# Turning the memory at a step's end in two parts, with the sum copied by ScalarE

## The chip, the cores and the metric

The kernel runs on one core of a Trainium2 chip. The metric is the device time of one execution in microseconds (us). The executions shown beside each other are of the same program on the same inputs; the figure is their median. One more execution was recorded by the hardware profiler, and all durations below come from that one.

The engines are TensorE (PE, with its weight loads listed apart as PEld), VectorE (DVE), ScalarE (ACT), GpSimd (POOL) and SyncE (SP). In this kernel SP only issues transfers of weights.

## The reference, cut to what matters

Two branches read the same x and are mixed by a gate. Branch A is attention in a sliding window of 256. Branch B runs over 64 segments of 32 tokens; each segment sees 8 memory rows that the segment before it has made, so the 64 steps follow one another.

```python
# S = 2048, Dm = 640, H = 32 heads, Dh = 192, M = 8 memory rows, seg_len = 32
mem = mem0
for s in range(n_seg):                                   # 64 steps
    xs = x[:, s * seg_len:(s + 1) * seg_len, :]
    h = concatenate([mem, xs], axis=1)                   # 40 rows x 640
    q, k, v = h @ Wq, h @ Wk, h @ Wv                     # 640 -> 32 heads x 192
    p = softmax(where(mask, q @ k.T * Dh ** -0.5, -1e9))
    o = (p @ v) @ Wo                                     # 40 rows x 640
    mem = o[:, :M, :]                                    # the next step's memory
    outs.append(o[:, M:, :])
return g * a + (1 - g) * concatenate(outs, axis=1)       # a: branch A, g: gate
```

## The kernel before, in words

Branch A comes first, and then the parts of branch B that need no memory. From about 434 us on the 64 steps run, the function branch_B.

All operations of all steps are first recorded by `sc.op(engine, duration, latency, function, reads, writes, ...)` in a planner, the class Sched. The order on PE is written out by hand: the string STEP names the work of one step, and it ends with "oa3 ob3 m", after which the next step's "k0 q0 k1 ..." begins. The order on SP is the order of recording. On DVE, ACT and POOL the planner chooses among ready operations by rank, with the duration and latency that were written beside each operation. The program is then emitted in that order. Each engine works through its own instructions in order.

The heads are worked in 4 groups of 8. For a group g the step has projections q, k and v (line 773), their turns tq and tk (line 797), scores s, the turn p of the probabilities, values pv, and the projection back, in two halves oa and ob (line 968). A projection is 5 pieces of the contraction, kt = 0 to 4, each with 4 small matmuls. Its stationary operand is `hT`, the step's input turned: 128 partitions x 5 pieces x 32 columns. Of a piece's 32 columns 0 to 7 are the memory rows and the others are tokens that a POOL transfer brings in (line 703). The last 8 tokens of a segment don't depend on the memory; their projections were made for all steps ahead.

[...]21 pieces a step, of 384 KB (q, k, v) or 320 KB (o), are streamed on SP's queue into a ring of 5 buffers, `b_w`. A transfer into a buffer is issued when PE has read the piece that lay there. The pieces read first in a step are one of k0, one of q0, one of k1 and one of q1.

The end of a step is a short serial path:

1. The projection back has summed into one PSUM bank, `ps_o`, 128 partitions x 320 in fp32: partitions 0 to 63 hold the columns 0 to 319 of o, partitions 64 to 127 the columns 320 to 639. The rows 0 to 7 of each half are the new memory.
2. DVE copies the sum into a bf16 tile, `osum` (line 977; the tile comes from the pool OT).
3. PE turns the memory rows by 10 small matmuls with an identity, 5 pieces x 2 halves, into a PSUM tile `mem_ps` (line 989, the operation "m" of STEP).
4. DVE copies `mem_ps` into columns 0 to 7 of all 5 pieces of the next step's `hT` (line 994).
5. PE begins k0 of the next step.

Beside this path POOL stores osum (line 999) and fetches branch A's rows `ga` (line 1000); DVE mixes both later (line 1004, placed by the planner after a copy of the next step), and POOL stores the result (line 1008). PSUM tiles of the pool "tr" have two buffers that the turns and `mem_ps` use in rotation.

Of the kernel before, what the change touches and what calls it, by code (L numbers as in the profile page):

```python
# [8 lines left out]
FP32 = mybir.dt.float32  # L9
BF = mybir.dt.bfloat16  # L10
ALU = mybir.AluOpType
ACT = mybir.ActivationFunctionType
# [3 lines left out]
MEM = 8  # L16
# [377 lines left out]
P = 128  # L394
KT = 5
D = 640
# [273 lines left out]
def branch_B(ctx, tc, xin, mem0, weights, ring, c, omg_sb, ga_dram, b_dram, outf, hold, held, rest):  # L670
    nc = tc.nc
    nseg = xin.shape[0]
    scale = float(192) ** -0.5
    still, ident, mask, mk_m, mk_x, mk_z = c.still, c.ident, c.mask, c.mk_m, c.mk_x, c.mk_z
    kept = KEPT

    sb = {
        "w": (RING, [P, PIECE]), "tok": (3, [P, 384]), "vtok": (1, [P, 384]), "K02": (1, [P, 4, 2, L]),
        "PTm": (1, [P, 2, 4, L]), "Pm": (1, [P, 4, SEG]), "xg": (2, [P, 2, 12, MEM]), "xv": (1, [P, 384]), "hT": (2, [P, KT, SEG]),
# [6 lines left out]
    sc = Sched({"rest": len(held)} | {t: n for t, (n, _) in sb.items()} | {t: n for t, (n, _) in kept.items()} | ps)  # L686

    def tile_of(b, shape=None, dtype=BF, name=None):
        t = b["tag"]
        if b["tile"] is None:  # L690
            if t in kept:
                b["tile"] = still[t][b["n"] % kept[t][0]]
            elif t in sb:
                b["tile"] = pools[t].tile(sb[t][1], BF, name=f"b_{t}", tag=t)
            else:
                b["tile"] = pools[t].tile(shape, dtype, name=name or f"p_{t}", tag=t)
        return b["tile"]

    def load_x(s):
        hb = sc.buf("hT")  # L700

        def f():
            nc.gpsimd.dma_start(tile_of(hb)[:].rearrange("p k t -> p (k t)"), xin[s, :, 0:KT * SEG])
        return hb, sc.op("POOL", 540, 5000, f, writes=[hb])
# [16 lines left out]
    def pieces(kind, g, ms=range(5)):  # L721

        out = {}
        for m in ms:
            u = (kind, g, m)
            if u in weights.streamed:
                b = out[m] = sc.buf("w")
                sc.op("SP", 0.753 * weights.width(kind), 3000, lambda b=b, u=u: weights.load(u, tile_of(b)[:, 0:weights.width(u[0])], nc.sync), writes=[b])
        return out

    def w_of(kind, g, m, bufs):
        return bufs[m]["tile"] if m in bufs else weights.tiles[kind, g, m]
# [15 lines left out]
    hts = {0: load_x(0)}  # L748
# [3 lines left out]
    def f_m0():  # L752
        t = tile_of(tp, [P, KT, MEM], BF, "tp0")
        for kt in range(KT):
# [4 lines left out]
          writes=[hts[0][0]], after=[hts[0][1]])  # L759
    made, tails = {}, {}  # L760

    def chunk(kind, s, g):
        if s == 0 and kind == "v":
            load_slow(g)
        hT = hts[s][0]
        b = sc.buf("mm")
        wb = pieces(kind, g)

        def f(kt):
            t = tile_of(b, [P, 512], FP32, f"ps_{kind}")  # L770
            w = w_of(kind, g, kt, wb)
            for j in range(4):
                nc.tensor.matmul(t[32 * j:32 * j + 32, 0:384], lhsT=tile_of(hT)[:, kt, :], rhs=w[:, j * 384:(j + 1) * 384],  # L773
                                 start=(kt == 0), stop=(kt == KT - 1), tile_position=(0, 32 * j))
        for kt in range(KT):
            sc.op("PE", 160, 330, lambda kt=kt: f(kt), reads=[hT] + [wb[m] for m in wb if m == kt], writes=[b], name=(kind, s, g, kt), mode=32)
        tok = sc.buf("vtok" if kind == "v" else "tok")

        def ev():
            src, dst = b["tile"][:, 0:384], tile_of(tok)[:]  # L780
            if kind == "v":
                src = src.rearrange("p (a e b) -> p a b e", a=2, b=3)
                dst = dst.rearrange("p (a b e) -> p a b e", a=2, b=3)
            nc.scalar.copy(dst, src)  # L784
        sc.op("ACT", 480, 50, ev, reads=[b], writes=[tok])
        made[kind, s, g] = tok
# [165 lines left out]
    def oproj(kind, s, g):  # L952

        ms = PARTS[kind]
        OT = made["O", s, g]
        if g == 0 and kind == "oa":
            obufs[s] = sc.buf("o")
        o_b = obufs[s]
        wb = pieces("o", g, ms)

        def f(m):
            t = tile_of(o_b, [P, 512], FP32, "ps_o")
            for n in range(2):
                i, b = divmod(2 * m + n, 3)
                c = (4 * b + i) * L
                for h in range(2):
                    w = w_of("o", g, m, wb)[:, n * D + h * (D // 2):n * D + (h + 1) * (D // 2)]
                    nc.tensor.matmul(t[64 * h:64 * h + 64, 0:D // 2], lhsT=OT["tile"][:, c:c + 64], rhs=w,  # L968
                                     start=(g == 0 and m == 0 and n == 0), stop=(g == 3 and m == 5 and n == 1),
                                     tile_position=(0, 64 * h), skip_group_check=True)  # L970
        for m in ms:
            sc.op("PE", 273, 200, lambda m=m: f(m), reads=[OT] + [wb[n] for n in wb if n == m] + [slow[u] for u in slow if s == 0 and u == ("o", g, m)],
                  writes=[o_b], name=("o", s, g, m), mode=64)
        if g < 3 or kind == "oa":
            return
        osum = sc.buf("OT")
        sc.op("DVE", 492, 55, lambda: nc.vector.tensor_copy(tile_of(osum)[:, 0:D // 2], o_b["tile"][:, 0:D // 2]), reads=[o_b], writes=[osum])  # L977
        made["osum", s] = osum

    def finish(s):  # L980

        osum = made.pop(("osum", s))
        b = sc.buf("tr")

        def f():
            t = tile_of(b, [P, KT, MEM], FP32, "mem_ps")
            for kt in range(KT):
                for h in range(2):
                    nc.tensor.matmul(t[64 * h:64 * h + 64, kt, :], lhsT=osum["tile"][:, kt:D // 2:KT], rhs=ident[:, 64 * h:64 * h + MEM],
                                     start=(kt == 0), stop=True, tile_position=(0, 64 * h), skip_group_check=True)  # L990
        sc.op("PE", 360, 222, f, reads=[osum], writes=[b], name=("m", s), mode=64)
        if s + 1 < nseg:
            hT, xl = hts[s + 1]
            sc.op("DVE", 200, 55, lambda: nc.vector.tensor_copy(tile_of(hT)[:, :, 0:MEM], b["tile"][:]), reads=[b], writes=[hT], after=[xl])
        ga, rows = sc.buf("ga"), slice(s * SEG, (s + 1) * SEG)
        half = lambda t, h: t[rows, h * (D // 2):(h + 1) * (D // 2)]
        mine = lambda t, h: t[64 * h + MEM:64 * h + L, 0:D // 2]
        for h in range(2):
            sc.op("POOL", 500, 3000, lambda h=h: nc.gpsimd.dma_start(half(b_dram, h), mine(osum["tile"], h)), reads=[osum])
            sc.op("POOL", 500, 5000, lambda h=h: nc.gpsimd.dma_start(mine(tile_of(ga), h), half(ga_dram, h)), writes=[ga])  # L1000

        def mix(after):
            def f_r():
                nc.vector.scalar_tensor_tensor(out=ga["tile"][:], in0=osum["tile"][:, 0:D // 2], scalar=omg_sb[:, s:s + 1], in1=ga["tile"][:],  # L1004
                                               op0=ALU.mult, op1=ALU.add)
            sc.op("DVE", 552, 60, f_r, reads=[osum], writes=[ga], after=[after])
            for h in range(2):
                sc.op("POOL", 500, 3000, lambda h=h: nc.gpsimd.dma_start(half(outf, h), mine(tile_of(ga), h)), reads=[ga])  # L1008
        made["mix"] = mix
        if s + 1 == nseg:  # L1010
            mix(None)
# [3 lines left out]
    for n in names:  # L1015
        kind, s = n[:2]
# [6 lines left out]
        elif kind in "qkv":  # L1023
            chunk(kind, s, n[2])
        elif kind in PARTS:
            oproj(kind, s, n[2])
        else:
            make[kind](s, n[2])
    with tc.manual_schedule():
        parts = []  # L1030
        for n in names:
            if n[0] in PARTS:
                parts += [("o",) + n[1:] + (m,) for m in PARTS[n[0]]]
            elif n[0] in KINDS:
                parts += [n + (m,) for m in range(KT)]
            else:
                parts.append(n)
        return sc.run([("m0", 0)] + parts)


PARTS = {"oa": range(3), "ob": range(3, 6)}
RING = 5
EARLY = 24
LAST = 11
# [9 lines left out]
def kernel(  # L1054
# [40 lines left out]
    units = [lambda u=u: weights.load_resident(pre, u, nc.sync) for u in early]  # L1095
    ring = wctx.enter_context(tc.tile_pool(name="b_w", bufs=RING))
    first = {}
# [78 lines left out]
    with ExitStack() as bctx:  # L1176
        rest = bctx.enter_context(tc.tile_pool(name="b_rest", bufs=1))
        branch_B(bctx, tc, xin, mem0, weights, ring, step_c, omg_sb, ga_dram, b_dram, outf, holds[0], last[HOLD:], rest)
# [41 lines left out]
```

## Time and profile before

| what | value |
|---|---|
| median of 5 executions | 2074.73 us |
| lowest and highest of them | 2064.33 and 2082.09 us |
| the profiled execution's own time | 2074.79 us |
| its span, first to last instruction | 2073.1 us |
| granted TensorE clock, mean over the span | 0.993 |
| busy share of the span: PE, DVE, ACT, POOL | 92%, 51%, 44%, 35% |
| bytes moved by the transfer engines | 593.83 MB, mean 286 GB/s |
| copy of the sum, DVE, line 977 | 64 times 492 ns |
| small products of the turn, PE, line 989 | 640 times, 217 ns each at the median, overlapping |
| copy into the next input, DVE, line 994 | 63 times 200 ns |

The span is nearly all of the profiled execution's time: 1.7 us lie around it. The profiled execution lies at the median of the others, so a difference worked out against the one may be read against the other.

How to read it: busy shares are means over the whole span, which holds branch A too. In the 64 steps PE and the transfer engines are both busy most of the time, and neither share says alone which one the end waits for. A matmul's own duration is longer than its share of the engine, since several are in flight at once.

### The profile page before, as it was taken

Reading aid. Unit: us, or ns where it says so; the run is one execution under the profiler, and the core shown is the slowest. Engines: PE = TensorE matmul, PEld = TensorE weight load, DVE = VectorE, ACT = ScalarE, POOL = GpSimd, SP = SyncE. Lnnn points to the kernel's source line nnn. Section 1 sums busy time; section 2 is a strip of 40 time slices with the busy share of each in tenths; the row PEclk is TensorE's granted clock in tenths of the full one; section 3 lists DMA queues with packets and bytes.
Section 4 is the critical chain, followed back from the end, with each engine's and each line's share of the span. In section 5 each row is a group of like instructions: output and inputs, shape, how many; then the busy total and the mean of one; then the engine's idle time right before and its main releaser. Section 6 shows DMA issues by size and latency. Waiting matters only on the chain.

```text
span 2073.1 us, 92142 instructions
## 1 busy us (share of the span) xinstructions
PE 1915.6 (92%) x39670; PEld 1410.8 (68%) x39670; DVE 1049.5 (51%) x3338; ACT 919.7 (44%) x1885; POOL 719.1 (35%) x2008
## 2 busy tenths in 40 slices
PE   7999999989999999999899999999999999989997
PEld 6878878756666666666666666666666666666665
DVE  4888853334444444445444444444444444444444
ACT  3788832234444444444444444444444444444443
POOL 4121121233334333333333333333333333333333
PEclk8999999999999999999999999999999999999999
DMA  4232149789999999999999999999999999999997
GB/s 137 78 89 69 45 109 349 205 285 327 333 323 333 328 322 320 329 326 333 320 332 331 321 331 326 327 332 334 331 314 337 327 318 337 333 323 318 332 330 263
DMA packets 251153, 593.83 MB, mean 286 GB/s; under 512 B 39528, under 2 KB 59120, under 8 KB 250736
## 3 DMA queue, kind: packets, MB, share of 16 engines
q1 hardware_dynamic: 219248, 540.07, 75.0%
q0 software_dynamic: 31488, 47.78, 8.7%
q8 instruction: 313, 5.13, 1.0%
q14 instruction: 104, 0.85, 0.1%
HBM read 558.33 MB, written 29.37 MB: 283 GB/s over the span
## 4 chain that ended last, share of the span: by engine, by line
PE 60%; DMA 25%; issue 7%; DVE 5%; ACT 3%; SPq 0%; POOL 0%; POOLq 0%; DVEq 0%; ACTq 0%
DMA b_w<-in_B_Wo_dram 10%; PE ps_q L773 10%; DMA b_w<-in_B_Wv_dram 10%; PE ps_k L773 10%; PE ps_o L968 8%; PE ps_v L773 6%; PE t_psum L584 4%; DMA b_w<-in_B_Wk_dram 4%; PE qk_ps L138 3%; PE t_psv L602 3%; PE tr_q L797 2%; PE S_ps L853 2%; PE tr_k L797 2%; PE s_ps L236 2%; PE ps_pv L935 2%
## 5 line engine op out<-in xcount | busy, mean ns | idle before, releaser
L773 PEld LDWEIGHTS <-b_hT 128*32 128x32 bf16 x15360 | 372.6, 96 | 273.6 <-issue 59.4
L968 PEld LDWEIGHTS <-b_OT 128*64 128x64 bf16 x6144 | 370.8, 110 | 57.7 <-issue 35.2
L784 ACT CAST b_tok<-ps_k 128x384 bf16<-128x384 f32 x256 | 122.4, 478 | 347.5 <-PE ps_k L773 338.8
L773 PE MATMUL ps_q<-w_q,b_hT 128*32 128x384 bf16 x4096 | 257.9, 329 | 2.1 <-issue 2.1
L773 PE MATMUL ps_k<-w_k,b_hT 128*32 128x384 bf16 x4096 | 245.6, 328 | 0.0
L968 PE MATMUL ps_o<-hold,b_OT 128*64 128x320 bf16 x2560 | 236.3, 300 | 0.0
L919 DVE TENSOR_TENSOR b_PTm<-PT_ps,marks 128x320 bf16<-128x320 f32 x256 | 125.9, 492 | 203.9 <-PE PT_ps L907 203.9
L968 PE MATMUL ps_o<-b_w,b_OT 128*64 128x320 bf16 x1792 | 206.4, 300 | 23.7 <-DMA b_w<-in_B_Wo_dram 22.0
L824 DVE TENSOR_TENSOR b_Kz<-tr_k,marks 128x256 bf16<-128x256 bf16 x256 | 108.1, 422 | 236.8 <-PE tr_k L797 230.7
L773 PE MATMUL ps_v<-w_v,b_hT 128*32 128x384 bf16 x3584 | 212.6, 327 | 0.0
L239 ACT ACTIVATE pt<-s_ps 128x1024 bf16<-128x1024 f32 x180 | 183.4, 1025 | 57.3 <-PE s_ps L236 54.3
L946 ACT CAST b_OT<-ps_pv 128x480 bf16<-128x480 f32 x256 | 142.9, 558 | 139.5 <-PE ps_pv L942 139.5
L784 ACT CAST b_vtok<-ps_v 128x384 bf16<-128x384 f32 x256 | 122.5, 478 | 158.8 <-PE ps_v L773 158.0
L718 POOL DMA_DIRECT2D b_xg<-xin x256 | 141.9, 554 | 83.5 <-POOL b_QT L810 51.4
L968 PE MATMUL ps_o<-w_o,b_OT 128*64 128x320 bf16 x1792 | 170.1, 300 | 0.0
L829 POOL COPY b_K<-b_xg 128x64 bf16<-128x64 bf16 x256 | 60.6, 237 | 306.9 <-PE S_ps L853 306.9
L806 ACT COPY b_QT<-tr_q 128x384 bf16<-128x384 bf16 x256 | 123.4, 482 | 87.8 <-PE tr_q L797 87.6
L784 ACT CAST b_tok<-ps_q 128x384 bf16<-128x384 f32 x256 | 122.9, 480 | 87.5 <-PE ps_q L773 87.2
L773 PE MATMUL ps_v<-b_w,b_hT 128*32 128x384 bf16 x1536 | 131.1, 331 | 30.8 <-DMA b_w<-in_B_Wv_dram 29.9
L1008 POOL DMA_DIRECT2D out_dram<-b_ga x128 | 63.5, 497 | 261.5 <-DVE b_ga L1004 251.7
L977 DVE CAST b_OT<-ps_o 128x320 bf16<-128x320 f32 x64 | 31.5, 492 | 212.3 <-issue 205.9
L797 PEld LDWEIGHTS <-b_tok 128*64 128x64 bf16 x3072 | 108.6, 111 | 41.4 <-issue 23.2
(141 smaller groups left out, 3712.0 us busy)
## 6 DMA issues: line engine op xcount, KB each, us to landing
b_w<-in_B_Wv_dram SPq DMA_DIRECT2D x384, 384.0 KB, 4.8
b_w<-in_B_Wo_dram SPq DMA_DIRECT2D x448, 320.0 KB, 4.8
b_w<-in_B_Wk_dram SPq DMA_DIRECT2D x256, 384.0 KB, 5.0
b_w<-in_B_Wq_dram SPq DMA_DIRECT2D x256, 384.0 KB, 5.1
xin<-hold POOLq DMA_DIRECT2D x8, 1536.0 KB, 11.9
b_xg<-xin POOLq DMA_DIRECT2D x256, 48.0 KB, 4.5
w_q<-in_B_Wq_dram SPq DMA_DIRECT2D x16, 384.0 KB, 3.8
w_k<-in_B_Wk_dram SPq DMA_DIRECT2D x16, 384.0 KB, 3.6
```

What stands on the lines that cost most here:

```text
L239: nc.scalar.activation(out=pt, in_=sp[:], func=ACT.Exp, scale=scale)
L584: self.nc.tensor.matmul(pt[:, bb, :], lhsT=w[kt][:, c:c + P], rhs=self.xTb[:, kt, t0:t0 + hs * MEM], start=(kt == 0), stop=(kt == KT - 1))
L718: sc.op("POOL", 540, 5000, lambda: nc.gpsimd.dma_start(tile_of(b)[:].rearrange("p i b t -> p (i b t)"), xin[s, :, c:c + 192]), writes=[b])
L773: nc.tensor.matmul(t[32 * j:32 * j + 32, 0:384], lhsT=tile_of(hT)[:, kt, :], rhs=w[:, j * 384:(j + 1) * 384], start=(kt == 0), stop=(kt == ...
L784: nc.scalar.copy(dst, src)
L797: nc.tensor.transpose(t[64 * a:64 * a + 64, k, :], tok["tile"][:, c:c + 64], ident[:], tile_position=(0, 64 * a))
L806: nc.scalar.copy(dst, tq["tile"][:].rearrange("p b (j t) -> p b j t", t=SEG))
L824: nc.vector.tensor_tensor(out=tile_of(Kz)[:, :, :, 0:SEG], in0=src, in1=mk_z.unsqueeze(1).unsqueeze(3).to_broadcast([P, 4, 2, SEG]), op=AL ...
L919: nc.vector.tensor_tensor(out=tile_of(PTm)[:], in0=src.to_broadcast([P, 2, 4, L]), in1=mk_m.unsqueeze(1).unsqueeze(3).to_broadcast([P, 2, ...
L946: sc.op("ACT", 560, 50, lambda: nc.scalar.copy(tile_of(OT)[:, 0:12 * L], o["tile"][:, 0:12 * L]), reads=[o], writes=[OT])
L968: nc.tensor.matmul(t[64 * h:64 * h + 64, 0:D // 2], lhsT=OT["tile"][:, c:c + 64], rhs=w, start=(g == 0 and m == 0 and n == 0), stop=(g == ...
L1008: sc.op("POOL", 500, 3000, lambda h=h: nc.gpsimd.dma_start(half(outf, h), mine(tile_of(ga), h)), reads=[ga])
```

## The change

The ten small products become two groups: the pieces 0 and 1 (4 products) and the pieces 2 to 4 (6 products), each into a PSUM tile of its own. Each group has its own DVE copy into its pieces of hT. The copy of the sum goes from DVE to ACT. The order on PE stays: both groups stand where the one group stood, between ob3 and the next k0.

```diff
         osum = sc.buf("OT")
-        sc.op("DVE", 492, 55, lambda: nc.vector.tensor_copy(tile_of(osum)[:, 0:D // 2], o_b["tile"][:, 0:D // 2]), reads=[o_b], writes=[osum])
+        sc.op("ACT", 430, 50, lambda: nc.scalar.copy(tile_of(osum)[:, 0:D // 2], o_b["tile"][:, 0:D // 2]), reads=[o_b], writes=[osum])
         made["osum", s] = osum
...
-        b = sc.buf("tr")
-
-        def f():
-            t = tile_of(b, [P, KT, MEM], FP32, "mem_ps")
-            for kt in range(KT):
-                for h in range(2):
-                    nc.tensor.matmul(t[64 * h:64 * h + 64, kt, :], lhsT=osum["tile"][:, kt:D // 2:KT], rhs=ident[:, 64 * h:64 * h + MEM],
-                                     start=(kt == 0), stop=True, tile_position=(0, 64 * h), skip_group_check=True)
-        sc.op("PE", 360, 222, f, reads=[osum], writes=[b], name=("m", s), mode=64)
-        if s + 1 < nseg:
-            hT, xl = hts[s + 1]
-            sc.op("DVE", 200, 55, lambda: nc.vector.tensor_copy(tile_of(hT)[:, :, 0:MEM], b["tile"][:]), reads=[b], writes=[hT], after=[xl])
+
+        def turn(i, kts):
+            b = sc.buf("tr")
+
+            def f():
+                t = tile_of(b, [P, KT, MEM], FP32, "mem_ps")
+                for kt in kts:
+                    for h in range(2):
+                        nc.tensor.matmul(t[64 * h:64 * h + 64, kt, :], lhsT=osum["tile"][:, kt:D // 2:KT], rhs=ident[:, 64 * h:64 * h + MEM],
+                                         start=(kt == kts[0]), stop=True, tile_position=(0, 64 * h), skip_group_check=True)
+            sc.op("PE", 72 * len(kts), 222, f, reads=[osum], writes=[b], name=("m", s, i), mode=64)
+            if s + 1 < nseg:
+                hT, xl = hts[s + 1]
+                c = slice(kts[0], kts[-1] + 1)
+                sc.op("DVE", 150, 55, lambda: nc.vector.tensor_copy(tile_of(hT)[:, c, 0:MEM], b["tile"][:, c]), reads=[b], writes=[hT], after=[xl])
+        for i, kts in enumerate(TURNS):
+            turn(i, kts)
...
+            elif n[0] == "m":
+                parts += [n + (i,) for i in range(len(TURNS))]
...
+TURNS = (range(2), range(2, KT))
```

## The prediction

> **What bounds the kernel now.** I read the windows of the steps first, for the balance of PE and transfers; then the timeline of one step's end; then the waits; then the chain of waits. In the windows view, columns are length, busy time by engine, granted clock, transfer share and GB/s.
>
> ```profile
> core 0: us, PE busy (x) PEld busy (x) DVE busy (x) ACT busy (x) POOL busy (x), PEclk, DMA share, GB/s
> 1736.37:1760.38 24.01, 23.07 (x526) 16.64 (x526) 12.17 (x43) 10.57 (x24) 9.63 (x29) 1.00 0.98 343
> ...
> 1530.09:1557.98 27.89, 25.06 (x526) 17.68 (x526) 12.17 (x43) 10.61 (x24) 9.63 (x29) 0.94 0.92 304
> ...
> 465.00:2065.00 1600.00, 1478.08 (x33109) 1059.92 (x33100) 766.53 (x2708) 666.51 (x1512) 601.83 (x1752) 1.00 0.96 327
> ```
>
> The first row is the shortest step, 24.01 us; the second the longest, at a lower clock. Over all of them PE is busy 1478 of 1600 us (92%) and the transfers hold 0.96. Both are near their ends. Every step has the same end, here one of them:
>
> ```profile
> 1022.73 0.44 PE L968 MATMUL ps_o<-b_w,b_OT 128*64 128x320 bf16 x4
> 1023.27 0.49 DVE L977 CAST b_OT<-ps_o 128x320 bf16<-128x320 f32 x1 [2.90 <-issue]
> 1023.81 0.46 PEld L989 LDWEIGHTS <-b_OT 128*64 128x64 bf16 x10 [0.97 <-DVE b_OT L977]
> 1023.81 0.54 PE L989 MATMUL mem_ps<-ident,b_OT 128*64 128x8 bf16 x10 [0.64 <-DVE b_OT L977]
> 1024.05 1.00 POOL L999 DMA_DIRECT2D b_dram<-b_OT  x2 [2.51 <-DVE b_OT L977]
> 1024.40 0.20 DVE L994 CAST b_hT<-mem_ps 128x40 bf16<-128x40 f32 x1 [0.64 <-PE mem_ps L989]
> ...
> 1024.65 0.35 PE L773 MATMUL ps_k<-b_w,b_hT 128*32 128x384 bf16 x4 [0.30 <-DVE b_hT L994]
> ```
>
> From the end of the last back projection (1022.73 + 0.44 = 1023.17) to the next k0 (1024.65) PE does nothing but ten small products: 1.48 us, 63 times, 93 us in all. The steps' waits say what else PE waits for:
>
> ```profile
> PE mem_ps L989 <- DVE b_OT L977: 40.8, 63, 1.0
> PE ps_v L773 <- DMA b_w<-in_B_Wv_dram: 26.7, 50, 1.7
> PE ps_o L968 <- DMA b_w<-in_B_Wo_dram: 21.5, 46, 1.5
> PE ps_k L773 <- DVE b_hT L994: 16.1, 54, 0.3
> PE ps_k L773 <- DMA b_w<-in_B_Wk_dram: 10.8, 13, 1.4
> ```
>
> Beside the step's end PE waits 26.7 + 21.5 + 10.8 = 59 us for weights, nearly 1 us a step. The shortest step has no such wait. So which one sets the end? The chain of waits through the steps passes the small products ("PE mem_ps L989") at 49 of the 63 ends. At the other 14 it goes past them through a weight transfer, mostly of Wk, issued before the step's end and landing behind it:
>
> ```profile
> 1249.03 7.34 DMA b_w<-in_B_Wk_dram
> 1256.37 0.04 issue
> 1256.41 0.51 PE ps_k L773 x8
> ```
>
> **The copy of the sum, from DVE to ACT.** DVE takes 492 ns for 320 columns. ACT's rows for fp32 from PSUM into bf16 are 478 ns for 384 columns (line 784) and 558 ns for 480 (line 946): 80 / 96 = 0.833 ns a column, so 478 - 64 x 0.833 = 425 ns for 320. The gain is 67 ns. From below ACT's 128x256 copy bounds it, 379 ns (line 568), from above the 478. The Trainium skill (VectorE: DVE Perf Modes, section on the TRN2 errata) gives for PSUM to SBUF 120 cycles + columns at 0.96 GHz on VectorE and 172 + columns at 1.2 GHz on ScalarE: 458 and 410 ns, a gain of 48. By the page this part is worth 63 x 48 = 3.0 us, by the rows 63 x 67 = 4.2; I take the rows. ACT is free: its last work before is line 946 at 1020.74 for 0.56, its next is line 784 at 1025.70. Behind the waiting copy on ACT stands only that evacuation of k0, which needs the copy anyway. ACT starts behind PE as soon as DVE does (0.04 us after ps_pv in the same step), and PE started 0.05 us behind ACT's line 946. POOL's stores of line 999 now wait for ACT and come 67 ns sooner; their order and SP's are unmoved.
>
> **The turn in two groups.** Ten products span 0.54 us, one 217 ns: (540 - 217) / 9 = 36 ns apart. Four of them end after 3 x 36 + 217 = 325 ns, 215 sooner than ten. The copy of 40 columns takes 200 ns, that of the sum 492 for 320: 292 / 280 = 1.04 ns a column and 158 fixed. 16 columns take 175 ns, 24 take 183. The first copy then ends 215 + 25 = 240 ns sooner. Counted from the first product (1023.81 in the example): first copy 0.38 to 0.55, k0 at 0.60 instead of 0.84. The second group is queued between, on PE, but is done at 0.54; the second copy starts behind the first at 0.59, ends at 0.77 and frees PE at 0.82. k0's pieces 0 and 1 need no more than the first copy; a piece takes 0.17 to 0.18 us, so piece 2 is due at 0.60 + 0.35 = 0.95. The second copy is covered by 0.13 us; without that cover it would cost what it is late, piece by piece. It is the thing that is late next. What the trace doesn't show is a wait in mid-group before piece 2 that is already met: at best 0, at worst the restart after a real wait, which I read from the chain: 20 products of k0 take 1.00 us behind the copy, of other groups 0.81, so 0.19. I take 0, since the loads run ahead of the products. The extra DVE copy (63 x 183 ns = 11.5 us busy) lies where DVE waits for tr_k for 3.01 us; it holds up nothing. The products and the pool "tr" get one more buffer use a step; the PSUM tile that the second group needs was last read at the turn of p3, over 3 us earlier.
>
> **The sum.** 67 + 240 = 307 ns an end, 63 x 0.307 = 19.3 us if every end counted. At the 14 ends that the chain passes by, nothing comes of it: 49 x 0.307 = 15.0 us. A step that starts sooner also finds its first four streamed pieces (k0, q0, k1, q1, within 3.3 us) landed later by comparison. Of them 13 products of k waited already. I let five more ends go that way, a choice, roughly one in ten of the 49: 44 x 0.307 = 13.5 us. 2074.8 - 13.5 = 2061.3; I say **2061 us**.
>
> The rule against it: the Trainium skill (Perfetto Trace Analysis, Identifying the Most-Contended Engine) would have one optimize the engine of the highest occupancy first. By that the transfers at 0.96 set the step and this change, which moves no byte less, gives 0: 2074.8. The rows say more. A mean step ((2040.2 - 463.8) / 62 = 25.43 us, from the first and the last copy of line 994) leaves 4% of transfer time idle, 1.0 us; the shortest leaves 2%, 0.5 us. 0.5 us can be taken up, more than 0.31. And the longest step has one of the lowest shares (0.92), which a pure limit of the transfers wouldn't give. So I take most of the sum, not all.
>
> **The rivals.** *Transfers hide it.* The saving turns into waits for weights, in the head of the step or at the v and o pieces, where most waits already are. For it: 0.96, and a wait in most steps. Against it: 49 of 63 ends on the chain. It gives 0 to 6 us: about 2071. *The halves aren't separate*: k0 waits for both copies after all, since hT is one tile. Then k0 starts at 0.82 instead of 0.84, 87 ns an end, 49 x 0.087 = 4 us: 2070.5. In the built program piece 2's load carries a wait of its own, so this is unlikely. *Broken heads*, the slower side: each of the first four streamed pieces that PE now overtakes costs a stall with its 0.19 us of restart. One stall takes back part, 0.307 / 0.19 = 1.6 new stalls a step take all; three would make 0.57 - 0.31 = 0.26 us a step, 63 x 0.26 = 16 us slower, 2091. For it: k products waited 13 times. Against it: q products waited once, and the shortest steps have none. *All of it counts*: 19.3 us, 2055.5.
>
> **How the numbers follow.** A change under 0.5% (10.4 us, so from 2064.4 to 2085.2) is about what a measurement here can't tell from none. Chances: the forecast 0.50 (2056 to 2067, six sevenths of it below 2064.4), all of it 0.10, hidden 0.20, not separate 0.05, broken heads 0.15. Faster 0.43 + 0.10 = 0.53; same 0.07 + 0.20 + 0.05 + 0.04 = 0.36; slower 0.11, since a mild form of broken heads stays within the bound. The range 2048 to 2080 leaves out most of broken heads and little else.
>
> **What would show it.** Line 977 on ACT at about 425 ns; two copies of 175 and 183 ns; from the last back projection to k0 1.17 us instead of 1.48; no idle time before piece 2 of k0; waits of PE for Wk above 13 but below 25, all weight waits up from 59 us by less than 6. The prediction is wrong if the gap at the end closes as said and the weight waits grow by 15 us or more (hidden), or if the gap stays above 1.35 us (not separate).

## The result, and the profile after

The changed kernel takes 2062.56 us (median of 42 runs, 2051.77 to 2078.44); the kernel before takes 2072.8 us (79 runs, 2058.58 to 2093.48). The ratio is 0.9951, 95% interval 0.9939 to 0.9963, which is 10.2 us less (7.7 to 12.6). That is 0.49%: a sure gain, though by a hair not one of more than 0.5%. By the plain means of all these runs it is 11.2 us (8.7 to 13.6).

The profiled execution of the changed kernel took 2048.3 us, 14 us below its median. That of the kernel before lay 2 us above its own. So the two spans, 2046.4 and 2073.1 us, must not be subtracted: of their 26.7 us only 10.2 are the change. What a profile does show well is what repeats 63 times alike, and that is the end of the step. First the timeline of one end in the changed kernel:

```profile
1014.52 0.47 PE L968 MATMUL ps_o<-b_w,b_OT 128*64 128x320 bf16 x4
1015.08 0.42 ACT L977 CAST b_OT<-ps_o 128x320 bf16<-128x320 f32 x1 [2.10 <-PE ps_o L968]
1015.55 0.46 PEld L991 LDWEIGHTS <-b_OT 128*64 128x64 bf16 x10 [0.89 <-ACT b_OT L977]
1015.56 0.54 PE L991 MATMUL mem_ps<-ident,b_OT 128*64 128x8 bf16 x10 [0.57 <-ACT b_OT L977]
1015.79 1.00 POOL L1004 DMA_DIRECT2D b_dram<-b_OT  x2 [2.58 <-ACT b_OT L977]
1015.91 0.41 DVE L997 CAST b_hT<-mem_ps 128x16 bf16<-128x16 f32 x2 [3.87 <-PE mem_ps L991]
...
1016.15 0.35 PE L773 MATMUL ps_k<-b_w,b_hT 128*32 128x384 bf16 x4
```

The ten products are shown as one run, since the second group starts without a gap. The two DVE copies are merged too (x2, 0.41 us from the start of the first). The first starts at 1015.91, before the products are through at 1016.10. k0 starts at 1016.15, while the second copy still runs to 1016.32. From the end of the back projection (1014.99) to k0 it is 1.16 us, and the median over the 63 ends is 1.163 us, where it was 1.485 before: 0.322 us an end, 63 x 0.322 = 20.3 us in all. **The kernel gained half of what its ends gained.**

The views of lines 977 and 997 give the durations (minimum, median, maximum):

```profile
L977 ACT CAST b_OT<-ps_o x64: 425/425/426, 463.6 to 2038.1; 128x320 bf16<-128x320 f32 x64
L997 DVE CAST b_hT<-mem_ps x126: 174/179/184, 464.4 to 2014.5; 128x16 bf16<-128x16 f32 x63, 128x24 bf16<-128x24 f32 x63
```

PE's waits in the changed kernel (total, times, longest):

```profile
PE mem_ps L991 <- ACT b_OT L977: 37.0, 64, 0.9
PE ps_v L773 <- DMA b_w<-in_B_Wv_dram: 23.3, 44, 3.2
PE ps_o L968 <- DMA b_w<-in_B_Wo_dram: 18.4, 42, 1.5
PE ps_k L773 <- DMA b_w<-in_B_Wk_dram: 7.8, 15, 1.2
PE ps_q L773 <- DMA b_w<-in_B_Wq_dram: 3.7, 9, 1.1
```

No row is left in which k0 waits for the copy into hT (54 such waits before). That doesn't mean that the copy no longer matters: it still stands inside the gap of 1.16 us, and the profile only doesn't name it any more. The q pieces at the head of a step were waited for once before and are now waited for 9 times, though this execution lies low among its kernel's. One end earlier than the one above, such a new wait is seen at k0 itself:

```profile
991.48 0.41 DVE L997 CAST b_hT<-mem_ps 128x16 bf16<-128x16 f32 x2 [3.74 <-PE mem_ps L991]
991.88 0.35 PE L773 MATMUL ps_k<-b_w,b_hT 128*32 128x384 bf16 x4 [0.21 <-DMA b_w<-in_B_Wk_dram]
```

Above, k0 starts 0.24 us after the first copy's start, here 0.40 us after it, because its own piece of weights lands only then. The shortest step tells more, in the windows view:

```profile
1342.78:1366.79 24.01, 23.34 (x532) 16.68 (x530) 11.84 (x44) 11.00 (x25) 9.63 (x29) 1.00 0.98 340
```

From the first copy into hT to the next step's first copy it is 24.01 us long at a transfer share of 0.98, exactly as the shortest step before, although each step has 0.322 us less of waiting in it. Three of its streamed pieces, one of v and two of o, are read 0.043 us after they land, which is the least that this trace has between a landing and the first product that reads the piece. The chain of waits can't be asked again in this trace, where the way back breaks off after 14 pieces, in the last step. In the trace of the split alone (below) it passes 41 of the 63 ends, where it passed 49 before.

### The profile page after: what moved, and what is told of

Same layout as the page of the kernel before. It is cut to its first block, busy times and chain, and to the rows that moved or that the text cites. A ratio compares the mean times of both kernels' runs of the same rounds, so it can differ in the third digit from the quotient of the medians.

```text
span 2046.4 us, 92206 instructions
## 1 busy us (share of the span) xinstructions
PE 1916.2 (94%) x39670; PEld 1411.5 (69%) x39670; DVE 1027.9 (50%) x3337; ACT 947.1 (46%) x1949; POOL 718.5 (35%) x2008
## 5 line engine op out<-in xcount | busy, mean ns | idle before, releaser
L968 PE MATMUL ps_o<-b_w,b_OT 128*64 128x320 bf16 x1792 | 206.4, 301 | 21.2 <-DMA b_w<-in_B_Wo_dram 18.4
L997 DVE CAST b_hT<-mem_ps 128x16 bf16<-128x16 f32 x126 | 22.5, 179 | 266.0 <-PE mem_ps L991 262.8
L797 PEld LDWEIGHTS <-b_tok 128*64 128x64 bf16 x3072 | 108.2, 110 | 40.7 <-issue 21.2
```

The lines of the kernel that those rows point to most:

```text
L797: nc.tensor.transpose(t[64 * a:64 * a + 64, k, :], tok["tile"][:, c:c + 64], ident[:], tile_position=(0, 64 * a))
```

## The experiments

The theory: PE's 20.3 us are real, and half of them are turned into waits for weights, since the transfers are nearly as full as PE. Rivals: half is lost elsewhere (clock, restarts of PE); one of the two parts brings it all; the transfers are a hard limit, so that more of them leave nothing. Where two runs are compared below, the difference is that of their means, with a 95% interval from the scatter of their runs.

**Without streamed weights: before and after.** The cut, the same for both kernels:

```diff
-            if u in weights.streamed:
+            if u in weights.streamed and u not in SKIP:
...
-        return bufs[m]["tile"] if m in bufs else weights.tiles[kind, g, m]
+        return bufs[m]["tile"] if m in bufs else weights.tiles[(kind, g, m) if (kind, g, m) in weights.tiles else ("q", 0, 0)]
...
+SKIP = {(k, g, m) for k in "qkvo" for g in range(4) for m in range(6)}
```

> The kernel before, but in the 64 steps no weight is streamed: every product that read a streamed piece reads one resident piece instead (so those 21 pieces a step are computed with other weights). Order on all engines as before. Theory (half of the shorter end was turned into waits for weights): PE sets the step alone, and every step takes what the shortest step took before, about 24.0 us; 63 x (25.43 - 24.0) = 90 us less, about 1983 us. No wait for weights is left in the steps. Rival (the end's saving is lost elsewhere, in the clock or in restarts of PE, and weights have little to do with it): the step stays above 24.3 us, and the time above 2003 us.

> The changed kernel with the same cut: no weight is streamed in the 64 steps, those products read one resident piece. Compared with the kernel before with this cut. Theory: with no weights to wait for, the end's whole 0.322 us comes through: 63 x 0.322 = 20.3 us less than the other cut kernel (17 to 22). Rival (half is lost elsewhere): 8 to 12 us less, as in the whole kernels. A second rival (the shorter end is only seen in the profile): 0 to 4 us less.

Measured: 1971.36 and 1950.39 us, 21.2 us apart (19.2 to 23.2). One step of each in the windows view, first the kernel before without streamed weights:

```profile
1125.09:1148.97 23.88, 22.94 (x526) 16.59 (x526) 12.17 (x44) 10.71 (x24) 9.28 (x28) 1.00 0.09 22
```

and the changed kernel without them:

```profile
1396.22:1419.77 23.55, 22.93 (x532) 16.58 (x530) 11.84 (x43) 11.12 (x25) 9.63 (x29) 1.00 0.09 23
```

The transfer share has fallen to 0.09, and the step goes from 23.88 to 23.55 us. From k0 to k0 the median of the 62 steps is 23.879 and 23.558 us, 0.321 apart. In the changed kernel with this cut PE waits for the sum's copy and for nothing else of size:

```profile
PE mem_ps L991 <- ACT b_OT L977: 37.0, 64, 0.9
PE S_ps L853 <- POOL b_QT L810: 1.0, 1, 1.0
```

So the end's whole 20.3 us comes through once no weights are streamed. Nothing that stays in these kernels takes the half. It isn't the clock either: these two profiles were granted 0.995 and 0.997, but the steps compared 1.00; and of the whole kernels the changed one had no lower clock, 0.993 in the mean of its runs against 0.992 over 45 runs of the kernel before.

The order of work is the same in both kernels of this pair, the change apart. It is not quite that of the whole kernels, though the expectation says so: PE's is, but with fewer transfers to place the planner exchanges some neighbours on DVE and ACT in every step. At one place this makes 0.12 us for PE. Without streamed weights the operation that writes the probabilities of one group (`b_Pm`) comes before the copies of K:

```profile
991.92 0.29 DVE L883 TENSOR_TENSOR b_Pm<-S_ps,sm 128x128 bf16<-128x128 f32 x1
992.68 0.43 DVE L824 TENSOR_TENSOR b_Kz<-tr_k,marks 128x256 bf16<-128x256 bf16 x1 [0.38 <-PE tr_k L797]
```

With 15 streamed pieces (a run further below) it comes behind them, as in the whole kernel:

```profile
1000.14 0.42 DVE L824 TENSOR_TENSOR b_Kz<-tr_k,marks 128x256 bf16<-128x256 bf16 x1 [0.15 <-PE tr_k L797]
1000.68 0.28 DVE L883 TENSOR_TENSOR b_Pm<-S_ps,sm 128x128 bf16<-128x128 f32 x1
```

PE's starts in the two steps, counted from k0, agree up to the turn of these probabilities and are 0.12 us apart behind it. So 24.00 is PE's own floor with that order and 23.88 with this one, and the 24.01 us of the shortest step before is as good as all PE's. The base came out 12 us below the 1983 expected for this reason and because the first step is shorter too (the second begins at 456.3 us, before at 464.0).

**The two parts alone, in the whole kernel and without streamed weights.** The first keeps the one group and moves the copy, the second keeps the copy on VectorE and splits the turn. For e7 and e8 the cut above is made as well:

```diff
# e3, e7: the kernel before with
-        sc.op("DVE", 492, 55, lambda: nc.vector.tensor_copy(tile_of(osum)[:, 0:D // 2], ...
+        sc.op("ACT", 430, 50, lambda: nc.scalar.copy(tile_of(osum)[:, 0:D // 2], ...
# e4, e8: the changed kernel with
-        sc.op("ACT", 430, 50, lambda: nc.scalar.copy(tile_of(osum)[:, 0:D // 2], ...
+        sc.op("DVE", 492, 55, lambda: nc.vector.tensor_copy(tile_of(osum)[:, 0:D // 2], ...
```

> The kernel before with the sum copied by ScalarE alone; the turn stays in one group. The end shrinks by 67 ns, 63 times, 4.2 us at most. Theory (about half of what the end gives comes through): 2 us less than before, not to be told from none. If the engine that copies is what brought the gain: 8 to 10 us less, ratio 0.995 to 0.996.

> The kernel before with the turn and its copies in two groups; the sum is still copied by VectorE. The end shrinks by 0.25 us, 63 times, 15.8 us at most. Theory (about half comes through): 8 us less than before, ratio 0.996. If the engine of the copy brought the gain: 0 to 2 us less, ratio 0.999 to 1.0.

> No weight streamed in the 64 steps (those products read one resident piece), and of the change only the copy by ScalarE. Against the 1971.4 us of the kernel before with that cut: the end is 71 ns shorter in the profile of the copy alone, 63 x 0.071 = 4.5 us less, 1967 us. If the two parts only bring their gain together: 0.

> No weight streamed in the 64 steps (those products read one resident piece), and of the change only the two groups with their copies. Against the 1971.4 us of the kernel before with that cut: the end is 0.254 us shorter in the profile of the split alone, 63 x 0.254 = 16.0 us less, 1955.4 us. A hidden stall before piece 2 would show as a smaller gain, 63 x 0.19 = 12 us less of it at worst, 1967 us.

In the whole kernel: the copy alone 2071.68 against 2076.98 us, ratio of the means 0.9979 (0.9949 to 1.0009); the split alone 2066.21, ratio 0.9966 (0.9937 to 0.9995). These intervals are as wide as the effects and don't tell the two apart. Without streamed weights they do: the copy alone 1967.04 us, 4.1 us less (-1 to 9), the split alone 1955.96 us, 15.3 us less (13 to 17.5). Expected were 4.5 and 16.0 from the ends in the profiles (1.485 to 1.414 us, and to 1.231). The parts add up, 4.1 + 15.3 = 19.4 beside 21.2 for both, and most of it is the split. These two ran on another chip than their base, and the whole kernel before differed by 2.3 us between the two chips; so the steps in the profiles are the better measure. From k0 to k0 the median is 23.879 us without the change, 23.812 with the copy alone, 23.629 with the split alone and 23.558 with both: 0.067 + 0.250 beside 0.321.

The profile of the split alone in the whole kernel shows the exchange, as its execution isn't far from its median:

```profile
PE ps_v L773 <- DMA b_w<-in_B_Wv_dram: 25.2, 41, 2.8
PE ps_o L968 <- DMA b_w<-in_B_Wo_dram: 25.1, 49, 1.6
PE ps_k L773 <- DMA b_w<-in_B_Wk_dram: 13.8, 17, 2.2
PE ps_q L773 <- DMA b_w<-in_B_Wq_dram: 3.2, 6, 1.0
```

The waits for weights are 67.3 us here and 62.9 in the kernel before over the same stretch (29.9 for v, 22.0 for o, 10.8 for k, 0.2 for q), with an end that is 16 us shorter in all. The head's pieces, k and q, rise from 11.0 to 17.0 us. These are single executions, and such sums move by several us from one to the next, so this shows where the waits appear, not how many us of them.

**Fewer streamed weights.** SKIP holds only the pieces of v: 15 of the 21 pieces stay.

> The kernel before without the six streamed pieces of v in the 64 steps (their products read a resident piece); the other 15 pieces are streamed as before. Transfers need about 24.4 - 6 x 1.16 = 17.4 us a step, PE 24.0. If a lack of transfer time makes the waits: few waits are left, 1971 to 1985 us. If the waits come from the time of one transfer through the ring, whatever the load: 2000 to 2040 us.

> The changed kernel without the six streamed pieces of v. Against the kernel before with this cut. Where few waits for weights are left, the end's gain comes through nearly whole: 17 to 21 us less. If half of it is lost as soon as weights are streamed at all: 8 to 12 us less.

Measured: 1983.37 and 1967.67 us, 16.4 us apart (13 to 20). PE waits for weights 1.5 us in all in the one and 1.4 in the other. So streaming as such doesn't cost the half: with a transfer share of 0.78 instead of 0.96 four fifths come through. It isn't quite the 17 to 21 expected, and about 4 us less than without streaming. The profiles show where these are. One usual step of each, from k0 to k0, the kernel before first:

```profile
989.52:1013.52 24.00, 23.06 (x526) 16.65 (x526) 12.16 (x43) 10.64 (x24) 9.62 (x29) 1.00 0.79 252
1075.35:1099.03 23.68, 23.06 (x527) 16.66 (x528) 11.82 (x44) 11.06 (x25) 9.66 (x29) 1.00 0.78 246
```

They are 0.32 us apart, the whole gain. In these two executions 54 of the 62 steps of the one and 42 of the other are such steps. The 8 later ones take 4.6 us more in all, the 20 later ones 8.8 us, and most of this difference arises at the streamed k and q pieces at the head.

**More streamed weights, and fewer buffers.** Two resident pieces are streamed as well, or the ring has 4 buffers:

```diff
-            if u in weights.streamed:
+            if u in weights.streamed or u in EXTRA:
...
+EXTRA = {("q", 3, 2), ("k", 2, 1)}
# and, in the other pair
-RING = 5
+RING = 4
```

> The kernel before with two more pieces of 384 KB streamed in every step (23 in place of 21), so that the transfers set the step. Before, a step took 24.37 us of transfer share at 25.43 us; two more pieces at 1.16 us each (384 KB at the 339 GB/s of the full stretches) make 26.7 us: 63 x (26.7 - 25.4) = 80 us more at least, about 2155 us or above, up to 2200. Both theories agree here; the run is the base of the next.

> The changed kernel with the same two more pieces streamed in every step. Compared with the kernel before with these pieces. Theory (what is lost of the end's gain is lost to the transfers): with the transfers setting the step nearly nothing comes through, 0 to 4 us less. Rival (a fixed half is lost whatever the transfers do): 10 us less. If the shorter end were worth all of it: 20 us.

> The kernel before with a ring of 4 buffers instead of 5. Four transfers in flight of about 5 us cover 21 pieces less well: each step waits some us more for weights, 2150 to 2350 us. The base of the next run.

> The changed kernel with a ring of 4 buffers. Against the kernel before with 4. The run with two more pieces lost no more of the gain than the whole kernel, so the transfers are no fixed limit. New theory: PE and transfers wait for one another in turn, and a transfer that is issued only when PE gives a buffer back inherits PE's delay, the end's included. With 4 buffers the transfers idle more and depend more on PE, so at least as large a part of 20.3 us comes through: 10 to 20 us less. Rival (the more PE waits for weights, the less comes through): 0 to 6 us less.

With two more pieces: 2218.82 (above the 2155 to 2200 expected) and 2202.2 us, 13.5 us apart (4 to 23). With 4 buffers: 2225.22 and 2221.33 us, 6 us apart (-4 to 16). Runs with long waits scatter by 10 us and more, and neither pair tells half from none or from nearly all. The first speaks against a loss of everything at a transfer share of 0.96, which the theory had expected; I had taken it for more than that when I wrote the expectations for 4 buffers, and these don't bear it out either way. What the first base does show: two more pieces cost 2218.8 - 2071.1 = 148 us, 63 steps x 2 x 1.17 us, the full time of each transfer at about 330 GB/s. With 21 pieces the kernel already stands where a further piece is paid in full.

**What is in flight at the end.** The trace of the kernel before allows an estimate that the prediction didn't make. SP's issues about the end that the prediction shows:

```profile
1019.22 0.33 SPq L517 DMA_DIRECT2D b_w<-in_B_Wk_dram  x1
1019.83 0.33 SPq L517 DMA_DIRECT2D b_w<-in_B_Wq_dram  x1
1021.00 0.33 SPq L517 DMA_DIRECT2D b_w<-in_B_Wk_dram  x1
1022.39 1.14 SPq L517 DMA_DIRECT2D b_w<-in_B_Wq_dram  x2
```

At all 63 ends the next step's first four streamed pieces (three with the ring of 4) are issued before the back projection ends (at 1023.17 here; of the last row the first issue). A shorter end can't make them land sooner. So the saving at an end can't be more than the time by which the tightest of the four lies ready before PE reads it, less the 0.043 us that always pass. Over the 63 ends this is 11.2 us of 20.3: 27 ends have room for all of it, 23 for less than 0.05 us. The same sum from the other bases' traces is in the table. It is an estimate: it takes each landing from one execution and lets the v and o pieces, which are issued later, move with PE.

| streamed pieces a step | transfer share in the steps, before | gain of the change, us | of the ends' 20.3 | estimate from the landings before, us |
|---|---|---|---|---|
| 0 | 0.09 | 21.2 (19.2 to 23.2) | all | 20.3 |
| 15 | 0.78 | 16.4 (13 to 20) | 0.8 | 18.6 |
| 21 (the whole kernel) | 0.96 | 10.2 (7.7 to 12.6) | 0.5 | 11.2 |
| 23 | 0.96 | 13.5 (4 to 23) | not settled | 12.6 |
| 21, ring of 4 | 0.92 | 6 (-4 to 16) | not settled | 8.0 |

The first three rows are the finding: the same edit, with the same shorter end, is worth less the fuller the transfers are. The estimate from the landings lies within the interval in every row, and it gives more for 23 pieces than for 21, so the transfer share alone need not set the order. The last two intervals are too wide to test that.

## Why the prediction was right, point by point

- **The direction and the size.** Forecast 13.5 us less, measured 10.2 (7.7 to 12.6). That 2061 us lies only 1.6 us beside the measured median is partly luck: the 2074.8 us that I counted from lay 2.0 us above the median of the 79 executions, and the gain was forecast 3.3 us too large.
- **The copy on ACT.** 425 ns forecast, 425 measured. The rows' slope was better than the 410 ns of the Trainium skill (VectorE: DVE Perf Modes, The TRN2 errata). The end shrank by 71 ns with this part alone, 67 forecast.
- **The split.** 175 and 183 ns forecast for the copies, 174 and 184 measured; the end shrank by 0.254 us with this part alone, 0.240 forecast. The gap after: 1.17 forecast, 1.163 measured.
- **The wait before piece 2**, whose price I took as 0: the 20 products of k0 take 0.996 us at the median both before and after, piece 2 starts 0.335 us behind k0's start in both, and without streamed weights the split shortens the step by 0.250 of the end's 0.254 us. It costs nothing that these runs can see. That the loads run ahead of the products shows at a back projection of the trace before, where they start at 1022.60 and the products at 1022.73. That k0 does not wait for both copies is shown by its start under the second copy, at 58 of 63 ends, so *not separate* falls.
- **How much comes through** is the term that was mis-sized. I took 44 of 63 ends as paid, 0.70; measured is 10.2 / 20.3 = 0.50 (0.38 to 0.62). The step that failed was to count the ends on the chain (49) and then to guess five off. The chain tells which wait came last at each end. It doesn't tell how late the next one was. At 22 of the 49 ends on the chain, and at all 14 off it, one of the four pieces in flight lay ready by less than the saving. By the landings the trace before held 11.2 us, as much as 35 whole ends, where I counted 44.
- **The rule to work on the fullest engine first** gave 0 and the chain 15.0. The measured 10.2 lies between, so neither stands alone. The 0 was my reading of the rule: the Trainium skill (Perfetto Trace Analysis, Identifying the Most-Contended Engine) ranks transfers by their use of the memory's bandwidth and not by the busy share of 0.96 that I put in, and it doesn't say that work elsewhere gives nothing. Its doubt was well placed: without the transfers the same edit is worth 21.
- **Room in the transfers.** I argued that 0.5 us of idle transfer time a step was room enough for 0.31. The shortest step with 21 pieces is 24.01 us in both kernels. With 15 pieces and few waits the usual step is 24.00 us before and 23.68 after. So before the change PE set the shortest step, and after it even the shortest step lies 0.33 us above what PE needs, with three pieces read as they land. On average there was room; this step had none.
- **Broken heads.** The head's waits grew as it said, q from 1 to 9 times. Their price was far from outweighing the end: from k0 to the first turn the mean is 2.72 us before, 2.71 after (in an execution that lies low) and 2.78 with the split alone.
- **The check by waits for weights** (up by less than 6 us) couldn't be made on the profile: it shows 53.2 us, fewer than before, in an execution 14 us below its kernel's median. In the profile of the split alone they rise by 4.4 us.

## What to carry to other kernels

When two resources are both above 90% busy, cut the serial part all the same, but expect only part of it: a chain through one trace says who came last, not by how much, so ask also how long the second waited. Here the transfers already issued at the end, set beside the times at which they are read, gave an estimate of 11 of the 20 us, from the trace before alone. To learn what an edit does by itself, take the other resource away in both versions; the scatter falls too, and four or six runs then give an effect of 15 or 20 us to within about 2 us, where twelve runs of the whole kernel leave 5 us or so each way. Never subtract two profiled spans when each kernel's own runs scatter by more than the effect.

## What was not expected of the hardware

- The scatter between executions is larger where the transfers are full: six runs of the kernel before lie within 5 us with no weights streamed (1969.79 to 1974.61), within 5 us with 15 pieces (1980.35 to 1985.37), and within 17 us with 23 (2208.73 to 2225.69). The cause is open, since the time goes with the granted clock as well: over 45 whole runs of the kernel before, at 0.986 to 0.996, a clock lower by 0.001 comes with about 2.1 us more.
- The time from a landing to the first product that reads the piece has a sharp lower end: 0.043 us, over all 1344 streamed pieces of either whole kernel's trace. So a piece that PE had to wait for can be told from one that lay ready, even where the list of waits has no row for it.
